# A chunked retention layer followed by a squared-ReLU channel mix: smaller chunks from block 3 on, another form of the token mix in four blocks, and a rewritten instruction order

## The chip, the core and the metric

The kernel runs on one core of a Trainium2 chip. That core has a matrix engine (TensorE, PE in the profile), a vector engine (VectorE, DVE), an activation engine (ScalarE, ACT), a general engine (GpSimd, POOL) and a queue engine (SyncE, SP) that only issues transfers. Each engine executes its own instructions strictly in program order and waits on semaphores for the others. Transfers between HBM and the on-chip memory (SBUF) are moved by 16 DMA engines; they can be issued from POOL (the profile's queue q0, software_dynamic), from SP (q1, hardware_dynamic) and from ACT (q10, hardware_dynamic). TensorE writes its results to PSUM, which has 8 banks.

The metric is the device time of one execution in microseconds. Before the change, three executions took 156.35, 156.45 and 157.85 us, median 156.45.

## What is computed

The first half is a recurrence over 768 tokens for 4 batches and 8 heads of width 64. A 64x64 state is decayed by a head's gamma, gains the outer product of k and v, and is read with q:

```python
gamma = 1.0 - 2.0 ** (-5.0 - np.arange(H))
for t in range(S):
    state = gamma * state + einsum('bhd,bhe->bhde', k[:, :, t], v[:, :, t])
    y[:, :, t] = scale * einsum('bhd,bhde->bhe', q[:, :, t], state)
```

The heads are joined to rows of 512 numbers, x, and the second half is a channel mix in which each token also sees the token before it:

```python
x_prev = x shifted by one token, zero at the start
xk = mu_k * x + (1 - mu_k) * x_prev
xr = mu_r * x + (1 - mu_r) * x_prev
out = sigmoid(xr @ w_r) * (max(xk @ w_k, 0) ** 2 @ w_v)
```

w_k is 512x1024, w_v is 1024x512, w_r is 512x512. Inputs and output are float32; the kernel feeds TensorE with float16.

## The kernel before

The tokens are cut into 12 blocks of 256 tokens; three blocks in a row (0 to 2, 3 to 5, 6 to 8, 9 to 11) belong to one batch and hand a state on. The recurrence is not stepped token by token. Inside a block it is done in chunks: scores of k against q within a chunk (S), a mask (M), the masked scores times v (Y), and what earlier chunks carry over (I and J read the carried states; C makes k times v per chunk, U adds it to the carried state, G applies a whole block's decay).

There are three layouts. Block 0 has 128-token chunks of interleaved tokens. Blocks named in WIDE (1 to 5) have two chunks of 128 tokens. Blocks named in HALF (6 to 11) have four chunks of 64 tokens; their scores are 64x64 pieces that use the four quarters of the matrix array, 32 matmuls a block (line 319), with one mask over the block (line 348) where a wide block has two (line 355). Blocks 0 to 5 turn q and k with 16 transposes of 128 rows each (line 273); blocks 6 to 11 with 32 transposes of 64 rows (line 279).

Every step is a short word in a string, ORDER (lines 23 to 75), which a loop at line 720 walks once. A word's code picks the function, its numbers the block and piece, the letter after ~ the engine (v DVE, a ACT, p POOL, s SP), the digits after @ the PSUM banks. So the order of the words is the order of work on every engine and in every queue; no scheduler moves anything, semaphores only add the waits that data and buffers need.

| word | what it does | line, engine |
|---|---|---|
| lq, lk, lv | load q, k, v of a block (k and v in two halves, except in block 0) | 231, 236, POOL or SP |
| wk, wr, wv | load the weights: wk.1 and wk.0 are the halves of w_k | 700, 703, 707, POOL |
| Tq, Tk; Eq, Ek | transpose q, k; copy the result out of PSUM | 273 or 279 PE; 242 ACT |
| vs | v times the decay factors | 254 DVE |
| S, M, Y, I, J, C, U, G | the chunked recurrence | PE; M, U DVE; G ACT or DVE |
| D | the block's x: PSUM times a decay table into xT | 508 or 515 DVE |
| dx, X | x minus shifted x; mu times that plus shifted x | 530, 539 DVE |
| K, Qa, Qb | w_k product; ReLU; square | 553 or 563 PE; 572, 580, 584 ACT |
| R, s | w_r product; sigmoid | 593 PE; 599 ACT |
| V, O, st | w_v product; times gate; store | 605 PE; 611 DVE; 618 SP |
| z | matmuls on a zero tile | 668, 675 PE |

X.n.w.j makes the j-th quarter of the channels of xk (w = 0) or xr (w = 1). K.n.g needs all four X.n.0.j. Products with w_k take columns 256g to 256g+255 in blocks that stand alone, so K.0.2 and K.0.3 need wk.1 (the second half), K.0.0 and K.0.1 need wk.0. Blocks (3, 4), (6, 7) and (9, 10) are joined for K; the others stand alone.

Buffers are reused in a ring: 4 for q, k and v each, so lv.4 must wait until vs.0 has read block 0's v. Each queue also has 8 semaphores for transfers in flight: a ninth is issued when the first of them has landed.

The order starts with the loads: SP issues the first halves of k and q of block 0; POOL issues the rest of block 0, then v, k, q of block 1, k and q of block 2, wk.1, wk.0, v of block 2, wr, and so on.

Of the kernel before, what the change touches and what calls it, by code (L numbers as in the profile page):

```python
# [22 lines left out]
ORDER = """  # L23
lk.0.0.2~s gy.0 lq.0.2.4~p lv.0~p lq.0.0.2~s lk.0.2.4~p ck.0.0.2~a z.12@6 Tk.0.0.2@0 mu
Tq.0.2.4@1 cq.0.0.2~a z.2@6 Tq.0.0.2@2 Ek.0.0.2~a vs.0~v Eq.0.0.2~a z.2@6 S.0.1.0.2@45
S.0.0.0.2@67 M.0.0.0.2~v Eq.0.2.4~a M.0.1.0.2~v Tk.0.2.4@2 Ek.0.2.4~a C.0@01 U.0.0~a U.0.1
S.0.0.2.4@67 M.0.0.2.4~v I.0@45 S.0.1.2.4@01 mt@3 me M.0.1.2.4~v lv.1~p vs.1~v gy.1~a G.0~a
z.4@2 Y.0 D.0~v lk.1~p Tk.1@0 Ek.1~a C.1@67 U.1.0 lq.1~p z.1@2 Tq.1@1 Eq.1~a dx.0~v X.0.0.0
z.4@2 S.1.1@01 lk.2~p I.1@45 S.1.0@23 M.1.1~v M.1.0~v lq.2~p Tq.2@6 Eq.2~a wk.1~p X.0.0.3 Tk.2@0
X.0.0.2 z.1@1 Y.1 J.1 X.0.0.1 D.1~v U.1.1 Ek.2~a z.1@2 S.2.1@01 S.2.0@23 K.0.2@6 dx.1~v K.0.3@4  # L30
Qa.0.3 Qa.0.2 wk.0~p z.2@5 K.0.1@7 Qa.0.1 K.0.0@5 Qb.0.2 X.0.1.0 X.1.0.2 lv.2~p Qa.0.0 Qb.0.1
X.1.0.3 wr~p X.1.0.1 X.1.0.0 K.1.2@4 lv.3~p G.1~a K.1.1@7 X.0.1.1 vs.2~v Qa.1.2 Qb.1.2 M.2.1~v
Qb.0.0 C.2@5 U.2.0 K.1.0@6 lq.3~p Qa.1.1 X.0.1.2 X.0.1.3 K.1.3@0 Qa.1.3 I.2@45 R.0.1@1 R.0.0@7
s.0.1 M.2.0~v Y.2 Qa.1.0 X.1.1.3 X.1.1.2 Qb.1.0 Tq.3@1 Eq.3~a J.2 X.1.1.0 X.1.1.1 R.1.0@6 s.0.0
# [44 lines left out]
def kernel(  # L79
# [625 lines left out]
    def load_wv(e, h):  # L705
# [59 lines left out]
```

## Time and profile before

The profiled execution took 156.1 us; its span, first to last instruction, was 154.3 us, so 1.8 us lie around it.

| | busy us | share of the span | instructions |
|---|---|---|---|
| PE | 147.3 | 95% | 2316 |
| DVE | 128.1 | 83% | 203 |
| ACT | 99.1 | 64% | 182 |
| POOL | 55.2 | 36% | 67 |

| transfers | packets | MB | share of 16 engines |
|---|---|---|---|
| q0, issued by POOL | 39920 | 14.95 | 75.2% |
| q1, issued by SP | 4512 | 6.69 | 11.9% |

How to read it: the page's part 2 cuts the span into 40 slices of 3.86 us and gives the busy tenths of each engine, so that stages can be told apart. The chain of work goes back from the last instruction through whatever released each step. The timeline gives start, length and name of instructions in order. Matmuls overlap in the records, so PE cost is read here from one piece's start to the next piece's start, not from the recorded length. Transfers have a time of issue and a time of landing; packets of a queue can overlap too, so a queue's share can be over 100% in a short window.

### The profile page before, as it was taken

What the parts mean: (1) busy time and instruction counts of PE and PEld (TensorE: products, weight loads), DVE (VectorE), ACT (ScalarE), POOL (GpSimd) and SP (SyncE); (2) the same over time, 40 slices, a digit from 0 to 9 for tenths busy, and PEclk for the clock granted to TensorE, in tenths of its full rate; (3) what the DMA queues carried; (4) which work ended last, traced back from release to release, by engine and by line L of the source; (5) the groups of instructions that cost most, each with busy time, mean ns of one, the idle gap of its engine ahead of it and who ended that gap; (6) DMA issues with size and microseconds to landing.
All of it is one profiled execution on the core that took longest, in us unless ns stands there. A gap on an engine that the chain in (4) does not pass through costs nothing.

```text
span 154.3 us, 5316 instructions
## 1 busy us (share of the span) xinstructions
PE 147.3 (95%) x2316; PEld 84.2 (55%) x2316; DVE 128.1 (83%) x203; ACT 99.1 (64%) x182; POOL 55.2 (36%) x67
## 2 busy tenths in 40 slices
PE   7979899999999999999999999999998999999991
PEld 3355668558744364556555455546664446455450
DVE  2499999989999999999999999999999996050531
ACT  3559338989872899657572799796411689449330
POOL 7998626788438849108960000000000000000000
PEclk9999999999999999999999999999999999999999
DMA  4999999999999999973999170000300015001435
GB/s 140 283 184 171 204 243 248 166 216 207 190 180 216 219 293 267 188 78 88 305 248 175 12 272 8 0 6 4 138 4 4 0 68 204 0 20 53 155 117 204
DMA packets 44903, 22.29 MB, mean 144 GB/s; under 512 B 36424, under 2 KB 40400, under 8 KB 44880
## 3 DMA queue, kind: packets, MB, share of 16 engines
q0 software_dynamic: 39920, 14.95, 75.2%
q1 hardware_dynamic: 4512, 6.69, 11.9%
q8 instruction: 18, 0.29, 0.8%
q10 hardware_dynamic: 448, 0.32, 0.7%
q14 instruction: 5, 0.04, 0.1%
HBM read 24.31 MB, written 6.29 MB: 198 GB/s over the span
## 4 chain that ended last, share of the span: by engine, by line
PE 42%; DVE 36%; issue 8%; POOL 6%; DMA 5%; ACT 3%; DVEq 0%; POOLq 0%
PE ps L605 13%; PE ps L553 9%; PE ps L593 8%; DVE xk L539 6%; PE ps L563 5%; DVE dx L530 5%; DMA q<-in_q_dram 5%; DVE xr L539 4%; DVE a L355 4%; DVE xT L515 3%; DVE vs L254 3%; DVE tg L420 3%; DVE os L611 2%; POOL k L231 2%; DVE xT L508 2%
## 5 line engine op out<-in xcount | busy, mean ns | idle before, releaser
L605 PE MATMUL ps<-wv,k2s 128*128 128x512 f16 x184 | 44.4, 380 | 0.0
L572 ACT ACTIVATE kr<-ps 128x512 f32<-128x512 f32 x48 | 27.8, 597 | 21.2 <-PE ps L563 11.7
L605 PEld LDWEIGHTS <-k2s 128*128 128x128 f16 x184 | 17.3, 98 | 18.8
L611 DVE SCALAR_TENSOR_TENSOR os<-ps,rs 128x512 f32<-128x512 f32 x23 | 15.1, 684 | 14.4 <-PE ps L605 7.9
L593 PE MATMUL ps<-wr,xr 128*128 128x512 f16 x96 | 23.9, 380 | 0.0
L231 POOL DMA_DIRECT2D v<-in_v_dram x22 | 19.8, 916 | 10.5 <-DVE vs L254 7.9
L563 PE MATMUL ps<-xk,wk 128*128 128x256 f16 x192 | 23.5, 273 | 0.0
L231 POOL DMA_DIRECT2D k<-in_k_dram x22 | 19.6, 905 | 10.5 <-DMA wk<-in_moe_w_k_dram 3.4
L553 PE MATMUL ps<-xk,wk 128*128 128x512 f16 x96 | 22.6, 379 | 0.8 <-DVE xk L539 0.8
L599 ACT ACTIVATE rs<-ps 128x512 f32<-128x512 f32 x24 | 14.1, 602 | 13.5 <-PE ps L593 9.4
L563 PEld LDWEIGHTS <-wk 128*128 128x128 f16 x192 | 18.2, 98 | 4.6 <-DMA wk<-in_moe_w_k_dram 0.5
L539 DVE SCALAR_TENSOR_TENSOR xr<-dx,mu,xT 128x256 f16<-128x256 f32 (+1 forms) x36 | 19.3, 566 | 0.0
L539 DVE SCALAR_TENSOR_TENSOR xk<-dx,mu,xT 128x256 f16<-128x256 f32 (+1 forms) x36 | 18.8, 567 | 0.2
L254 DVE TENSOR_TENSOR vs<-v,csm_sb 128x1024 f16<-128x1024 f32 x12 | 14.6, 1216 | 2.1 <-DMA v<-in_v_dram 2.1
L553 PEld LDWEIGHTS <-wk 128*128 128x128 f16 x96 | 9.0, 98 | 12.1 <-DVE xk L539 1.1
L242 ACT COPY kT<-ps 128x1024 f16<-128x1024 f16 (+1 forms) x13 | 12.2, 951 | 4.4 <-PE ps L279 3.3
L584 ACT ACTIVATE k2s<-kr 128x512 f16<-128x512 f32 x24 | 14.8, 632 | 0.2
L530 DVE TENSOR_TENSOR dx<-xT 128x1024 f32<-128x1024 f32 x12 | 14.6, 1219 | 0.2
L580 ACT ACTIVATE k2s<-kr 128x512 f16<-128x512 f32 x24 | 14.7, 629 | 0.1
L355 DVE TENSOR_TENSOR a<-ps,c_sb 128x1024 f16<-128x1024 f32 (+1 forms) x14 | 14.4, 1062 | 0.0
L242 ACT COPY qT<-ps 128x1024 f16<-128x1024 f16 (+1 forms) x13 | 12.3, 954 | 3.2 <-PE ps L273 2.9
L593 PEld LDWEIGHTS <-xr 128*128 128x128 f16 x96 | 8.7, 98 | 9.7
(67 smaller groups left out, 154.3 us busy)
## 6 DMA issues: line engine op xcount, KB each, us to landing
out_dram<-os SPq DMA_DIRECT2D x23, 256.0 KB, 2.6
v<-in_v_dram POOLq DMA_DIRECT2D x22, 256.0 KB, 7.0
k<-in_k_dram POOLq DMA_DIRECT2D x23, 128.0 KB, 7.4
q<-in_q_dram POOLq DMA_DIRECT2D x11, 256.0 KB, 7.8
wk<-in_moe_w_k_dram POOLq DMA_DIRECT2D x2, 512.0 KB, 10.2
wv<-in_moe_w_v_dram POOLq DMA_DIRECT2D x2, 512.0 KB, 10.0
v<-in_v_dram POOLq DMA_DIRECT2D x1, 512.0 KB, 5.6
wr<-in_moe_w_r_dram POOLq DMA_DIRECT2D x1, 512.0 KB, 13.1
```

The lines of the kernel that those rows point to most:

```text
L231: e.dma_start(out=dst[:, :, i * D : i * D + D], in_=src[:, i * P : i * P + P].rearrange("h p d -> p h d"),)
L242: e.copy(out=out, in_=in_)
L254: e.tensor_tensor(out=VS(n), in0=V32(n).rearrange("p h (i d) -> p i h d", i=2), in1=gks[:, int(half(n) or wide(n)), :, :, None].to_broadca ...
L355: nc.vector.tensor_tensor(out=a_full(n)[:, i, :, j0:j1], in0=pairs(banks("S", n, i, j0))[:, :, j0:j1], in1=(below if wide(n) else causal[: ...
L530: e.tensor_tensor(out=DX(k)[:, :, m * TM + t0 : m * TM + t1], in0=x[:, :, c + t0 : c + t1], in1=x[:, :, c - 1 + t0 : c - 1 + t1], op=ALU.s ...
L539: nc.vector.scalar_tensor_tensor(out=XM[w](k)[:, j, t0:t1], in0=DX(k)[:, j, t0:t1], scalar=mu[:, w * NCO + j : w * NCO + j + 1], in1=x[:, ...
L553: nc.tensor.matmul(banks("K", n, g), lhsT=wk16[:, co, g * P : g * P + P], rhs=XM[0](k)[:, co, :], start=(co == 0), stop=(co == NCO - 1),)
L563: nc.tensor.matmul(pz[:, i, :], lhsT=wk16[:, co, fo * P : fo * P + P], rhs=XM[0](k)[:, co, m * TM + t0 : m * TM + t1], start=(i == 0 and c ...
L572: nc.scalar.activation(out=kr, in_=banks("K", n, g, *u), func=AF.Relu)
L593: nc.tensor.matmul(banks("R", n, tb), lhsT=XM[1](k)[:, co, t : t + P], rhs=wr16[:, co, :], start=(co == 0), stop=(co == NCO - 1),)
L605: nc.tensor.matmul(banks("V", n, tb), lhsT=K2(n)[:, fo, tb * P : tb * P + P], rhs=wv16[:, fo, :], start=(fo == 0), stop=(fo == NFO - 1),)
L611: nc.vector.scalar_tensor_tensor(out=OS(2 * n + tb), in0=banks("V", n, tb), scalar=1.0 / (KSC * KSC), in1=RS(2 * n + tb), op0=ALU.mult, op ...
```

## The change

- HALF becomes blocks 3 to 11 and WIDE blocks 1 and 2: blocks 3, 4 and 5 go from two 128-token chunks to four of 64. WHOLE becomes blocks 0 to 2, so 3, 4 and 5 also take the 32 transposes of 64 rows.
- In blocks 0, 1, 2 and 5 (PARTED) the word dx is gone. For each quarter and each of xk, xr a new word ax lets ScalarE write (1 - mu) times the shifted x, and X computes mu times x plus that. A second small constant, nu = 1 - mu, is made once.
- ORDER is new throughout. Among the loads, v of blocks 0 to 5, 10 and 11 is issued by SP instead of POOL (8 blocks; ~s), and on POOL the order at the start becomes half of k of block 0, q of block 1, half of q of block 0, k of 1, q of 2, k of 2, wk.1, wk.0.
- G of blocks 0, 3 and 9 moves from ACT to DVE, G of block 6 from DVE to ACT, U.9.0 from DVE to ACT. There are 7 z words instead of 9.

```diff
-HALF = (6, 7, 8, 9, 10, 11)
+HALF = (3, 4, 5, 6, 7, 8, 9, 10, 11)
...
-WHOLE = (0, 1, 2, 3, 4, 5)
-WIDE = (1, 2, 3, 4, 5)
+WHOLE = (0, 1, 2)
+WIDE = (1, 2)
+PARTED = (0, 1, 2, 5)
...
 ORDER = """
-lk.0.0.2~s gy.0 lq.0.2.4~p lv.0~p lq.0.0.2~s lk.0.2.4~p ck.0.0.2~a z.12@6 Tk.0.0.2@0 mu
...
+lk.0.2.4~p lq.0.0.2~s cq.0.0.2~a z.8@7 Tq.0.0.2@0 Eq.0.0.2~a lq.1~p lk.0.0.2~s ck.0.0.2~a z.5@1
+Tk.0.0.2@1 Ek.0.0.2~a z.3@2 S.0.1.0.2@23 gy.0 lv.0~s Tk.0.2.4@1 vs.0~v lv.1~s M.0.1.0.2~v mu
+Tq.1@0 C.0@45 vs.1~v lq.0.2.4~p S.0.0.0.2@67 Ek.0.2.4~a M.0.0.0.2~v U.0.0~a lk.1~p z.1@1
+Tq.0.2.4@1 Eq.0.2.4~a z.3@2 I.0@23 S.0.0.2.4@67 U.0.1 Eq.1~a G.0~v M.0.0.2.4~v lq.2~p lk.2~p
+S.0.1.2.4@45 M.0.1.2.4~v Tk.1@1 C.1@67 U.1.0 U.1.1 Y.0 I.1@45 gy.1~a D.0~v wk.1~p Ek.1~a
+S.1.1@67 G.1~a mt@1 me ax.0.0.3 Tq.2@0 S.1.0@23 ax.0.0.1 M.1.1~v ax.0.1.0 ax.0.0.0 M.1.0~v
+X.0.0.3 Tk.2@1 ax.0.1.1 X.0.0.0 Ek.2~a ax.0.0.2 z.4@6 Y.1 J.1 X.0.0.2 wk.0~p X.0.0.1 Eq.2~a
+z.1@6 S.2.1@67 S.2.0@23 K.0.3@0 D.1~v K.0.2@1 M.2.0~v ax.0.1.2 ax.0.1.3 ax.1.0.1 X.1.0.1 lv.2~s
...
     def whole(n):
-        return n in WHOLE or n in WIDE
+        return n in WHOLE
...
+    def kept(n, w, j):
+        return DX(place[n][0])[:, j, w * TM : w * TM + TM]
+
+    def keep(e, n, w, j):
+        x, c = col(n)
+        nc.scalar.activation(
+            out=kept(n, w, j), in_=x[:, j, c - 1 : c - 1 + TM], func=AF.Copy,
+            scale=nu[:, w * NCO + j : w * NCO + j + 1],
+        )
+
     def mixed(e, n, w, j, i=None):
...
+        if n in PARTED:
+            nc.vector.scalar_tensor_tensor(
+                out=XM[w](k)[:, j, 0:TM], in0=x[:, j, c : c + TM],
+                scalar=mu[:, w * NCO + j : w * NCO + j + 1], in1=kept(n, w, j),
+                op0=ALU.mult, op1=ALU.add,
+            )
+            return
```

More of the change, by code (lines that the diff above doesn't have):

```diff
@@ L16 @@
 KUP = 4.0
-HALF = (6, 7, 8, 9, 10, 11)
+HALF = (3, 4, 5, 6, 7, 8, 9, 10, 11)
 EARLY = ((1, 0, 0), (0, 0, 0))
 GROUPS = ((0,), (1,), (2,), (3, 4), (5,), (6, 7), (8,), (9, 10), (11,))
-WHOLE = (0, 1, 2, 3, 4, 5)
-WIDE = (1, 2, 3, 4, 5)
+WHOLE = (0, 1, 2)
+WIDE = (1, 2)
+PARTED = (0, 1, 2, 5)
+WKP = 2
 HEADS = ((0, 1), (3, 2), (4, 5), (7, 6))
 ORDER = """
-lk.0.0.2~s gy.0 lq.0.2.4~p lv.0~p lq.0.0.2~s lk.0.2.4~p ck.0.0.2~a z.12@6 Tk.0.0.2@0 mu
-Tq.0.2.4@1 cq.0.0.2~a z.2@6 Tq.0.0.2@2 Ek.0.0.2~a vs.0~v Eq.0.0.2~a z.2@6 S.0.1.0.2@45
@@ new lines @@
+S.1.1@67 G.1~a mt@1 me ax.0.0.3 Tq.2@0 S.1.0@23 ax.0.0.1 M.1.1~v ax.0.1.0 ax.0.0.0 M.1.0~v
+X.0.0.3 Tk.2@1 ax.0.1.1 X.0.0.0 Ek.2~a ax.0.0.2 z.4@6 Y.1 J.1 X.0.0.2 wk.0~p X.0.0.1 Eq.2~a
+z.1@6 S.2.1@67 S.2.0@23 K.0.3@0 D.1~v K.0.2@1 M.2.0~v ax.0.1.2 ax.0.1.3 ax.1.0.1 X.1.0.1 lv.2~s
+ax.1.0.0 X.1.0.0 ax.1.0.2 X.1.0.2 ax.1.1.1 Qa.0.2 ax.1.0.3 X.1.0.3 ax.1.1.0 lk.3~p K.0.0@4
+Qb.0.2 Qa.0.3 Qa.0.0 ax.1.1.2 K.0.1@1 lq.4~p K.1.3@2 vs.2~v C.2@0 Qa.0.1 Qb.0.0 wr~p K.1.1@3
+X.1.1.1 Qb.0.3 X.0.1.0 lv.3~s U.2.0 M.2.1~v I.2@45 Qb.0.1 Qa.1.1 K.1.2@0 Qa.1.2 X.0.1.1 X.0.1.3
@@ new lines @@
+ax.1.1.3 Qa.1.3 K.1.0@6 X.0.1.2 lq.3~p Qa.1.0 Y.2 X.1.1.2 Tk.3@01 J.2 Ek.3~a X.1.1.0 Tq.4@23
+X.1.1.3 Eq.4~a D.2~v R.0.1@6 ax.2.0.2 ax.2.0.1 R.0.0@7 R.1.0@2 lv.4~s vs.3~v s.0.1 C.3@01
+Tq.3@45 X.2.0.2 X.2.0.1 ax.2.0.0 X.2.0.0 R.1.1@6 ax.2.0.3 X.2.0.3 K.2.3@3 U.3.0~a U.3.1 U.3.2
+lk.4~p U.3.3 vs.4~v s.1.0 Eq.3~a I.3@45 S.3@01 s.1.1 K.2.2@6 Qb.1.1 Qa.2.3 G.3~v C.4@23 s.0.0
+Qb.1.0 Qb.1.2 wv.0~p Qa.2.2 M.3~v wv.1~p ax.2.1.2 K.2.1@7 Tk.4@01 Ek.4~a Y.3 Qa.2.1 U.4.0 U.4.1
+K.2.0@6 U.4.2 I.4@01 U.4.3 G.4~a S.4@23 lk.6~p D.3~v Qb.1.3 M.4~v V.1.0.0@7 V.0.0.0@4 Y.4 Qa.2.0
@@ new lines @@
+Qb.2.0 dx.3~v D.4~v dx.4~v V.1.1.0@6 ax.2.1.1 lq.7~p V.0.1.0@5 ax.2.1.0 lk.5~p V.1.1.1 lq.5~p
+Qb.2.1 Tk.6@23 Ek.6~a X.3.0.2 X.3.0.3 X.3.0.0 Tq.7@01 V.1.0.1 V.0.0.1 X.3.0.1 V.0.1.1 O.1.0
+Eq.7~a O.0.0 Qb.2.3 Tk.5@23 Ek.5~a Tq.5@01 Eq.5~a K.3.3@7 lv.5~s vs.5~v lq.6~p K.3.1@4 Qb.2.2
+K.3.6@2 Qa.3.3 C.5@01 Qa.3.6 O.0.1 O.1.1 Tq.6@67 Eq.6~a K.3.4@5 X.2.1.2 U.5.0 U.5.1 U.5.2 lk.7~p
+X.2.1.1 S.5@23 Qa.3.1 M.5~v Tk.7@67 S.6@01 M.6~v V.2.1.0@4 Ek.7~a I.5@23 Qa.3.4 Qb.3.1 Qb.3.4
+lk.8~p S.7@67 M.7~v ax.2.1.3 K.3.2@5 Qb.3.6 Qa.3.2 V.2.1.1 X.3.1.1 lq.8~p Tq.8@01 lv.6~p X.2.1.0
@@ new lines @@
+Tk.8@67 Qb.3.3 X.2.1.3 Ek.8~a Y.5 Qb.3.2 K.3.7@5 R.2.0@6 D.5~v ax.5.0.2 lv.7~p Eq.8~a lv.8~p
+s.2.0 Qa.3.7 vs.6~v X.3.1.3 R.2.1@2 K.3.0@3 st.0.0 Qa.3.0 st.0.1 X.3.1.2 C.6@01 U.6.0~a
+V.2.0.0@5 X.3.1.0 lk.9~p ax.5.0.3 K.3.5@3 s.2.1 Qb.3.0 U.6.1 U.6.2 vs.7~v Qa.3.5 Qb.3.7 V.2.0.1
+R.3.0@3 U.6.3 ax.5.0.0 O.2.0 st.2.0 G.6~a X.5.0.2 O.2.1 st.2.1 R.4.1@2 s.3.0 X.5.0.0 lq.11~p
+s.4.1 C.7@67 I.6@01 U.7.0 U.7.1 U.7.2 ax.5.0.1 X.5.0.1 X.5.0.3 U.7.3 Tk.9@45 Ek.9~a lq.9~p
+V.3.1.0@3 R.4.0@2 I.7@45 Y.6 vs.8~v G.7~a s.4.0 D.6~v lv.10~s dx.6~v K.5.0@7 K.5.3@6 lq.10~p
@@ new lines @@
+Qb.3.5 V.4.0.0@2 ax.5.1.3 C.8@01 Y.7 D.7~v dx.7~v U.8.0 X.6.0.0 U.8.1 Qa.5.0 Qb.5.0 st.1.1
+st.1.0 X.6.0.3 X.6.0.2 ax.5.1.0 U.8.2 V.3.0.0@7 V.3.0.1 O.3.0 V.4.1.0@4 V.4.1.1 ax.5.1.1 O.4.1
+ax.5.1.2 X.6.0.1 Qa.5.3 R.3.1@5 s.3.1 Qb.5.3 K.5.2@1 Qa.5.2 Qb.5.2 K.5.1@5 Qa.5.1 V.3.1.1 O.3.1
+lv.11~s I.8@01 st.3.1 X.5.1.3 S.8@67 Tq.9@45 lk.10~p Eq.9~a V.4.0.1 M.8~v K.6.3@3 Qb.5.1 st.3.0
+Qa.6.3 Tq.10@45 Eq.10~a Tk.10@67 O.4.0 Ek.10~a Y.8 lv.9~p V.5.0.0@2 V.5.0.1 Tq.11@45 Eq.11~a
+S.10@67 vs.9~v D.8~v C.9@01 X.5.1.0 K.6.2@3 X.5.1.2 X.5.1.1 M.10~v Qa.6.2 st.4.1 K.6.6@4 K.6.1@3
@@ new lines @@
+K.6.4@5 vs.10~v Qb.6.2 X.6.1.2 X.6.1.1 Qa.6.1 Qa.6.6 R.5.0@3 U.9.0~a lk.11~p U.9.1 U.9.2 Qb.6.1
+s.5.0 dx.8~v O.5.0 U.9.3 X.6.1.3 Qa.6.4 Qb.6.4 V.5.1.0@4 G.9~v R.5.1@0 s.5.1 V.5.1.1 O.5.1
+Tk.11@67 C.10@23 S.9@01 Ek.11~a K.6.5@5 Qa.6.5 Qb.6.5 X.6.1.0 X.8.0.1 M.9~v K.6.0@6 Qa.6.0
+R.6.0@5 s.6.0 U.10.0 U.10.1 R.7.0@4 s.7.0 R.6.1@5 s.6.1 U.10.2 U.10.3 I.10@67 X.8.0.0 S.11@01
+st.4.0 I.9@23 X.8.0.2 X.8.0.3 Qb.6.6 R.7.1@4 s.7.1 K.6.7@5 M.11~v Qa.6.7 K.8.0@4 Qa.8.0 vs.11~v
+Y.9 D.9~v Y.10 D.10~v C.11@01 K.8.2@4 G.10~v U.11.0 dx.10~v dx.9~v X.9.1.2 Qb.6.3 X.8.1.2
@@ new lines @@
+K.8.1@5 Qb.6.7 Qb.6.0 V.6.1.0@2 V.7.0.0@3 V.6.0.0@6 V.6.0.1 K.8.3@7 Qa.8.1 X.9.0.2 Qa.8.2
+V.7.1.0@4 V.7.1.1 V.7.0.1 X.9.0.0 Qa.8.3 Qb.8.0 Qb.8.1 O.6.0 U.11.1 Qb.8.2 X.9.0.1 V.6.1.1
+X.9.0.3 Qb.8.3 V.8.0.0@5 K.9.3@6 Qa.9.3 X.8.1.3 X.9.1.3 K.9.0@7 K.9.2@6 X.9.1.1 Qa.9.0 K.9.6@7
+X.9.1.0 O.6.1 K.9.4@2 Qa.9.6 st.5.0 O.7.0 K.9.5@7 Qa.9.5 R.9.0@3 K.9.1@7 st.5.1 O.7.1 R.10.0@4
+U.11.2 I.11@01 Qb.9.3 Qa.9.2 K.9.7@6 st.6.1 X.8.1.1 Qb.9.2 Qa.9.1 Qb.9.1 Qa.9.7 X.8.1.0 st.7.0
+V.8.1.0@7 Qb.9.6 R.8.0@6 Y.11 s.9.0 V.8.0.1 Qb.9.0 V.9.1.0@3 Qa.9.4 st.7.1 Qb.9.5 R.9.1@2 s.8.0
@@ new lines @@
+D.11~v Qb.9.4 V.8.1.1 R.10.1@6 dx.11~v R.8.1@0 X.11.1.1 X.11.0.0 X.11.1.0 s.8.1 X.11.0.3
+V.10.0.0@1 X.11.0.1 X.11.0.2 st.6.0 X.11.1.2 O.8.0 X.11.1.3 V.9.0.0@0 K.11.1@5 s.10.0 Qb.9.7
+s.9.1 Qa.11.1 K.11.3@4 V.10.1.0@5 st.8.0 O.8.1 K.11.0@2 st.8.1 V.9.0.1 V.9.1.1 Qa.11.3 Qb.11.3
+O.9.1 Qa.11.0 Qb.11.0 O.9.0 st.9.0 K.11.2@4 Qa.11.2 Qb.11.2 V.10.0.1 st.9.1 O.10.0 st.10.0
+R.11.1@4 s.10.1 Qb.11.1 V.10.1.1 O.10.1 st.10.1 V.11.0.0@6 R.11.0@7 s.11.0 V.11.0.1 s.11.1
+O.11.0 st.11.0 Vc.11.1.0@7 Oc.11.1.0 Vc.11.1.1@4 Oc.11.1.1 sc.11.1.0~s sc.11.1.1~a
@@ L164 @@
     mu = const.tile([P, 2 * NCO], F32, name="mu")
+    nu = const.tile([P, 2 * NCO], F32, name="nu")
     wk16 = const.tile([P, NCO, dff], F16, name="wk16")
@@ L663, in copy_mu @@
         nc.scalar.copy(out=mu, in_=banks("mt")[:, 0 : 2 * NCO])
+        if PARTED:
+            nc.scalar.activation(out=nu, in_=mu, func=AF.Copy, scale=-1.0, bias=1.0)
     def zeros(e, count):
@@ L698, in load_wk @@
     def load_wk(e, h):
-        f = slice(h * dff // 2, (h + 1) * dff // 2)
+        f = slice(h * dff // WKP, (h + 1) * dff // WKP)
         nc.gpsimd.dma_start(out=wk16[:, :, f], in_=wks[:, :, f])
@@ L713 @@
         "S": scores, "M": masked, "C": state, "U": summed, "G": decayed, "I": inter_off, "Y": intra, "J": inter_on,
-        "D": yout, "dx": differ, "X": mixed, "K": keys, "Qa": relued, "Qb": squared, "R": gate,
+        "D": yout, "dx": differ, "ax": keep, "X": mixed, "K": keys, "Qa": relued, "Qb": squared, "R": gate,
         "s": opened, "V": values, "O": result, "st": store, "gy": powers, "wk": load_wk,
```

49 lines of the change are left out of this document (removed).

## The prediction

> **What bounds the kernel now.** I read the slices first, to see when each engine is full.
>
> ```profile
> PE   7979899999999999999999999999998999999991
> DVE  2499999989999999999999999999999996050531
> ACT  3559338989872899657572799796411689449330
> DMA  4999999999999999973999170000300015001435
> ```
>
> A slice is 3.86 us. Transfers fill the first 17 slices (66 us), VectorE nearly everything to slice 32, TensorE everything from slice 5. Next the timeline of PE where its solid stretch begins, and POOL's:
>
> ```profile
> 17.24 0.64 PE L273 MATMUL ps<-c_sb,q 128*64 128x128 f16 x16 [0.70 <-DMA q<-in_q_dram]
> ...
> 20.45 1.92 PE L563 MATMUL ps<-xk,wk 128*128 128x256 f16 x16
> 22.21 0.59 PE L675 MATMUL ps<-zero 128*128 128x512 f16 x2
> 22.80 3.67 PE L563 MATMUL ps<-xk,wk 128*128 128x256 f16 x32
> ```
>
> ```profile
> 20.09 0.88 POOL L231 DMA_DIRECT2D k<-in_k_dram  x1 [1.35 <-DMA wk<-in_moe_w_k_dram]
> 23.04 0.88 POOL L231 DMA_DIRECT2D k<-in_k_dram  x1 [2.07 <-DMA wk<-in_moe_w_k_dram]
> ```
>
> K.0.2 and K.0.3 start at 20.45, after wk.1 has landed (19.79); then zeros bridge until wk.0 lands (22.75) and K.0.1 starts at 22.80. From there the next pieces follow each other to 151.16: the idle marks on PE add up to under 1 us. So two things set the time: **when wk.0 lands, and how much PE work comes after it**. The 3.1 us behind PE's end (gate, store) stay as they are.
>
> **Smaller chunks: PE loses 2.8 us.** I sum, for a block's Tq, Tk, S, C, Y, I and J, the time from each piece's start to the next piece's start.
>
> ```profile
> 34.57 0.64 PE L273 MATMUL ps<-c_sb,k 128*64 128x128 f16 x16
> 44.85 0.44 PE L279 MATMUL ps<-c_sb,q 64*64 64x64 f16 x32
> ```
>
> These two lines are one turned block each: 0.57 us to the next piece when wide, 0.28 to 0.43 when half. All pieces: wide blocks 3, 4 and 5 take 2.95, 2.99 and 2.73 us; half blocks with the same place in their batch (6, 7, 8) take 1.90, 1.85 and 2.08. Saved: 8.67 - 5.83 = 2.84 us, all behind 22.8 and on the path, since PE is solid there.
>
> **VectorE loses 5 us.** Four dx at 1.22 (-4.9); in three blocks one mask of 1.21 instead of two (-3.6); six more U at 0.42 (+2.5); three D as 2 x 0.69 instead of 1.22 (+0.5); G net two more at 0.42 (+0.8); U.9.0 goes (-0.4). DVE is as full as PE to 117 us, so it must lose about what PE loses if PE's saving is to count; it does.
>
> **ScalarE gains 10.5 us.** 32 ax. The trace has no Copy of 128x256 with a scale; Copies with a scale take 348 ns for 64 columns (G) and 391 for 128 (the decay table), so 477 for 256 by that slope, and 0.38 as the engine advances, since its instructions overlap by 0.1 (G: four in 1.06). 32 x 0.38 = 12.2; two G fewer, -2.1; U.9.0, +0.4. It has 99 of 154 now. The new wait is X for its ax, which stands behind Qa, Qb and E in ACT's line; behind an X on DVE wait the next X, vs.2 and M.2.1. From 20 to 40 us ACT is busy 16.5 of 20; ax of blocks 1 and 2 (16, 6.1) less G.1 and G.3 (2.1) makes 20.5. So ACT is 0.5 us short there if block 0's keys start on time, up to 2 if its order fits badly; if they start late, ax.0 and most of ax.1, ordered before Qa.0.2, are done in the wait and this costs nothing.
>
> **The loads: wk.0 comes later.** POOL's transfers run one after another; landing to landing before: half k of block 0 0.61, lq.1 1.44, lk.1 1.15, lq.2 1.37, lk.2 2.43, wk.1 2.59, wk.0 2.96, and half q of block 0 as half of lq.1, 0.72. Now these eight are POOL's first: 10.31 us to wk.1, 13.27 to wk.0. v of a block took 1.86, 2.46, 1.84 and 2.26, mean 2.1. In the old order only v of 0 and 1 stood before wk.0. Now SP issues v of 0, 1, 2 and 3 without waiting for any compute, and 4 and 5 after vs.0 and vs.1: 12.6 us of transfers that are under way while wk is. What SP's small pieces cost the trace does not show: 33 ns per piece per engine (its q and k of block 0, 512 bytes each, 243 GB/s) would give 4.2 us for the 2048 pieces of a halved v block; k's pieces on POOL go at 13 ns, which gives 1.7. I take 2.1, POOL's own v.
>
> Do the two queues add up or share? Transfers between 58.6 and 59.8 us, when stores from SP met k from POOL:
>
> ```profile
> q0 software_dynamic: 774, 0.10, 130.1%
> q1 hardware_dynamic: 103, 0.19, 41.5%
> ```
>
> That is 645 k packets and 86 store packets per us. Alone, k runs at 1226 per us (10 to 11 us) and stores at 210 (90 to 92 us). 645/1226 + 86/210 = 0.53 + 0.41 = 0.94: they share, SP gets about 0.4. [...]
>
> With SP's share h, POOL's packets starting at 4.1 us and SP's v at 4.6 (when its q and k are through): wk.0 lands at 4.1 + 13.27/(1-h), v of 1 at 4.6 + 4.2/h. From v of 1, DVE must do, by start-to-start steps before, vs.1 1.23, M.0.0 0.6, U 0.34, G 0.36, two M 1.2, two U 0.66, D.0 1.15, two M 2.27, four X 1.66 = 9.5 us to K.0.3, and K.0.3 and K.0.2 1.75 more to K.0.0.
>
> | h | wk.0 | v of 1, + 11.25 | K.0.0 | against 22.80 |
> |---|---|---|---|---|
> | 0.25 | 21.8 | 21.4, 32.6 | 32.6 | +9.8 |
> | 0.35 | 24.5 | 16.6, 27.8 | 27.8 | +5.0 |
> | 0.40 | 26.2 | 15.1, 26.4 | 26.4 | +3.6 |
> | 0.45 | 28.2 | 13.9, 25.2 | 28.2 | +5.4 |
> | 0.50 | 30.6 | 13.0, 24.2 | 30.6 | +7.8 |
>
> 0.4 is the best for the new order, and either side is worse. I take 0.45, between the measured 0.4 and an equal share: **+5.4**. Later loads are not late: wr needs 5.8 us after wk.0 (lk.3, lq.4, wr), and PE has 7 us between K.0.0 and R.0.1.
>
> **The sum.** 156.1 (the profiled execution) - 2.8 + 5.4 = 158.7; that execution is 0.35 under the median, so **159.0** beside the runs shown. Its own range: 156.9 + 0.35 = 157.2 at h = 0.4, 161.3 at 0.5, up to 163.5 at 0.25 or with v pieces dearer than 2.1. One per cent, what a measurement of this kernel can tell from no change, is 154.9 to 158.0.
>
> **Rivals.**
>
> *The loads fit in, and it is faster.* v on SP could ride where POOL's small packets leave the engines' data path empty: k moves only 155 GB/s, stores alone 381. Then wk.0 and v of 1 land as before, K.0.0 starts at 22.8, and PE's 2.8 us come through: 153.3 + 0.35 = 153.7, with ACT's 0.5 154.2. It decides if wk.0 lands before 24.4. Against it stands the 0.94. Chance 0.25, 152.8 to 154.9.
>
> *Nearly balanced.* h close to 0.4 with POOL at its best pace, or PE stalls of the old order (under 1 us) also gone: 156 to 157.5. Chance 0.14, within 1%.
>
> *SP starves.* From 54 to 55 us, with k in full flow, SP's first store moved 21 packets against 761. If each 256-byte piece of v takes a turn of its own and lets 7.5 (the 58.6 to 59.8 ratio) to 36 k packets by, 2048 pieces take 12 to 60 us while POOL has work; POOL has 26.8 us of it that waits for no v but block 0's (to wv.1). v of 1 lands at 27 to 35, the keys start 15 to 23 us late, and the time is 169 to 177. For it: a lone store took longer beside loads.
>
> ```profile
> out_dram<-os SPq DMA_DIRECT2D x2, 256.0 KB, 5.0
> ```
>
> That is the median from issue to landing between 54 and 60 us; between 90 and 92, with no loads, it is 2.8. Against it: the 0.4 share afterwards. [...] Chance 0.13 with everything above 163.5.
>
> **Chances.** The forecast 0.48, faster 0.25, balanced 0.14, starved 0.13. Slower by over 1%: 0.48 + 0.13 = 0.61; within: 0.14; faster: 0.25. The range goes from 152.8 to 165: it leaves out most of the starved case and a little at the fast end.
>
> **What would show it.** Landing of wk.0 near 28 and an idle PE before K.0.0 prove the shared engines; PE waiting for vs.1 or X instead means the starved side. From K.0.0 to PE's end the time should be 128.4 - 2.8 = 125.5 us; more means that ACT or DVE became the bound, to be seen as PE waiting for X or for a freed bank. The prediction is wrong if wk.0 lands before 24.4.

## The result, and the profile after the change

The changed kernel takes **173.48 us** (median; 172.55 to 175.63), beside 157.15 us for the kernel before: ratio 1.10, 95% interval 1.089 to 1.113. It is slower by 16.3 us; 159.0 was forecast and 165.0 was the end of the range. Its profiled execution took 173.35 us with a span of 171.6; before it was 156.1 and 154.3. So 17.3 us are to be found. Executions more than 1.5% above the fastest of the same kernel count as a slower state, and the times of the versions below are medians of the others, which makes 173.4 for the changed kernel.

The slices of the changed kernel (now 4.29 us each), with the granted clock:

```profile
PE   7828869894996989788999699999999999999991
DVE  2243894799296899696999979999989990492431
ACT  3506475999399547696989267687672448918630
PEclk9985587998799999999999999999999999999999
DMA  5999999999999999899599904203000023003153
```

Three things are new. TensorE has holes in the first 23 slices, where it was solid from slice 5 on. Transfers fill 23 slices almost without a break (98 us), where before they filled 17 (66 us) and came in bursts after that; the last load packet starts at 99.8 instead of 86.5. And the granted clock, which was 1.0 in the kernel before, is low in slices 3 to 7 and in 10 and 11. The next fence is the timeline of PE about the first products; x16, x8 and so on count matmuls, and the bracket gives the idle time in front and what ended it.

```profile
29.55 1.92 PE L585 MATMUL ps<-xk,wk 128*128 128x256 f16 x16
31.68 1.05 PE L585 MATMUL ps<-xk,wk 128*128 128x256 f16 x8 [0.21 <-DMA wk<-in_moe_w_k_dram]
33.09 1.91 PE L585 MATMUL ps<-xk,wk 128*128 128x256 f16 x16 [0.36 <-ACT kr L594]
...
42.31 4.25 PE L615 MATMUL ps<-wr,xr 128*128 128x512 f16 x12 [2.21 <-ACT dx L545]
```

The first product starts at 29.55 instead of 20.45, and K.0.0 waits for wk.0. At 42.31 R.0.1 waits 2.2 us; the bracket names a scaling that ended then, but wr landed at 42.26 as well, and in three of the runs below the same wait is marked wr. Its first seven matmuls run at clock 0.5, 427 ns apart instead of 216: another 1.5 us. POOL's timeline shows the landings of wk.1 and wk.0 as the end of POOL's own waits, 28.3 and 31.6 against 19.8 and 22.8 before:

```profile
28.53 0.87 POOL L236 DMA_DIRECT2D k<-in_k_dram  x1 [2.44 <-DMA wk<-in_moe_w_k_dram]
31.92 0.75 POOL L731 DMA_DIRECT2D wv<-in_moe_w_v_dram  x1 [2.52 <-DMA wk<-in_moe_w_k_dram]
```

Then comes what no step of the prediction had. Further on in PE's timeline pieces are cut in two, and what lies between is marked "issue": the engine waited for nothing that the profile shows.

```profile
55.71 0.28 PE L447 MATMUL ps<-qT,tg 64*64 64x64 f16 x10 [1.70 <-issue]
...
62.18 0.32 PE L284 MATMUL ps<-c_sb,k 64*64 64x64 f16 x15 [0.59 <-issue]
...
67.55 1.69 PE L575 MATMUL ps<-xk,wk 128*128 128x512 f16 x7 [0.29 <-issue]
...
72.38 0.22 PE L284 MATMUL ps<-c_sb,k 64*64 64x64 f16 x3 [0.91 <-issue]
```

Two more follow at 77.75 and 95.87. From the start of the last matmul in front to the next one they are 1.89, 0.78, 0.66, 1.10, 1.37 and 1.98 us, 7.8 in all; the kernel before has none. I counted TensorE's instructions (matmuls and weight loads, by start time) up to each: 1473, 1729, 1985, 2241, 2497 and 3265. The first five are **256 apart**, the last is three times 256 further on. And each stall ends 2.3 to 2.7 us after the start of a packet of 16384 bytes in queue q8, "instruction". The first of these packets, in the transfers from 53 to 55.5 us:

```profile
q0 software_dynamic: 2394, 0.41, 211.2%
q8 instruction: 1, 0.02, 2.3%
```

The columns are packets, MB and the time of the packets as a share of the 16 engines. Loads fill all engines twice over (211.2%, packets overlap), and the one packet of q8 goes among them. That such a packet brings TensorE's next 256 instructions is read from counts: 20 of them came for the 5204 matmuls and weight loads of the changed kernel, 260 a packet, and 18 for the 4632 of the kernel before, 257 a packet; and the stalls stand 256 or a multiple of it apart. The kernel before takes its 18 packets without a stall; the changed kernel stalls at six of 20.

The 17.3 us are split by two marks: the first product starts 9.1 us later (29.55 against 20.45), from there to PE's end it takes 138.6 us instead of 130.7 (+7.9), and the tail is 0.3 longer. In the +7.9 stand the stalls (about 7.3 beyond the normal step), wr (2.2), the slow clock (1.5) and K.0.1's wait (0.4), together 11.4, against smaller chunks (-2.8, the size forecast). That makes 8.6, 0.7 more than was measured; what gives it back I cannot name.

### The profile page after: what moved, and what is told of

Same layout as the page of the kernel before. It is cut to its first block, busy times and chain, and to the rows that moved or that the text cites. A ratio compares the mean times of both kernels' runs of the same rounds, so it can differ in the third digit from the quotient of the medians.

```text
span 171.6 us, 5909 instructions
## 1 busy us (share of the span) xinstructions
PE 151.1 (88%) x2602; PEld 85.3 (50%) x2602; DVE 124.1 (72%) x206; ACT 110.6 (64%) x208; POOL 41.6 (24%) x52
## 4 chain that ended last, share of the span: by engine, by line
PE 70%; DMA 10%; ACT 6%; issue 5%; DVE 4%; POOL 3%; ACTq 0%; DVEq 0%; POOLq 0%
PE ps L627 24%; PE ps L615 12%; PE ps L575 12%; DMA k<-in_k_dram 10%; PE ps L585 8%; PE ps L284 3%; ACT dx L545 2%; PE ps L447 2%; PE ps L468 2%; PE ps L372 1%; POOL k L236 1%; POOL q L241 1%; PE ps L324 1%; ACT kr L594 1%; PE ps L692 1%
## 5 line engine op out<-in xcount | busy, mean ns | idle before, releaser
L627 PEld LDWEIGHTS <-k2s 128*128 128x128 f16 x184 | 17.3, 98 | 20.1 <-issue 1.9
L615 PE MATMUL ps<-wr,xr 128*128 128x512 f16 x96 | 25.0, 398 | 2.2 <-ACT dx L545 2.2
L575 PE MATMUL ps<-xk,wk 128*128 128x512 f16 x96 | 23.2, 380 | 0.3 <-issue 0.3
L259 DVE TENSOR_TENSOR vs<-v,csm_sb 128x1024 f16<-128x1024 f32 x12 | 14.6, 1217 | 8.3 <-DMA v<-in_v_dram 8.3
L513 DVE TENSOR_TENSOR xT<-ps,gy_sb 128x512 f32<-128x512 f32 x18 | 12.4, 690 | 9.5 <-PE ps L447 8.1
L615 PEld LDWEIGHTS <-xr 128*128 128x128 f16 x96 | 9.5, 102 | 14.3 <-DMA wr<-in_moe_w_r_dram 2.3
L545 ACT ACTIVATE dx<-xT,nu 128x256 f32<-128x256 f32 x32 | 14.7, 506 | 2.7 <-DVE xT L520 2.3
L425 DVE TENSOR_TENSOR tg<-ps,tg 128x256 f16<-128x256 f32 x26 | 11.0, 422 | 4.1 <-ACT tg L247 1.6
L241 POOL DMA_DIRECT2D q<-in_q_dram x12 | 10.5, 890 | 10.6 <-PE ps L284 7.5
L353 DVE TENSOR_TENSOR a<-ps,c_sb 128x1024 f16<-128x1024 f32 x9 | 11.0, 1219 | 2.4 <-PE ps L324 2.4
```

The costliest lines, as they stand in the source:

```text
L259: e.tensor_tensor(out=VS(n), in0=V32(n).rearrange("p h (i d) -> p i h d", i=2), in1=gks[:, int(half(n) or wide(n)), :, :, None].to_broadca ...
L545: nc.scalar.activation(out=kept(n, w, j), in_=x[:, j, c - 1 : c - 1 + TM], func=AF.Copy, scale=nu[:, w * NCO + j : w * NCO + j + 1],)
L575: nc.tensor.matmul(banks("K", n, g), lhsT=wk16[:, co, g * P : g * P + P], rhs=XM[0](k)[:, co, :], start=(co == 0), stop=(co == NCO - 1),)
L615: nc.tensor.matmul(banks("R", n, tb), lhsT=XM[1](k)[:, co, t : t + P], rhs=wr16[:, co, :], start=(co == 0), stop=(co == NCO - 1),)
L627: nc.tensor.matmul(banks("V", n, tb), lhsT=K2(n)[:, fo, tb * P : tb * P + P], rhs=wv16[:, fo, :], start=(fo == 0), stop=(fo == NFO - 1),)
```

## The experiments

Theory A has two parts: v on SP delays the weights, and TensorE's instruction packets wait behind loads, which small matmuls turn into stalls. The rivals are the scalings on ScalarE, the order by itself, and, for the stalls, the number of small matmuls alone. All numbers together; "first" is the start of the first product, "stretch" the time from there to PE's end, "stalls" the gaps of 0.5 us and more behind the first product that stand at the count of a 256-block and end 2.2 to 2.8 us after the start of its packet.

| kernel | time us | ratio (95%) | first | stretch | stalls |
|---|---|---|---|---|---|
| before | 157.2 | | 20.5 | 130.7 | 0 |
| after | 173.4 | 1.089 to 1.113 | 29.6 | 138.6 | 7.8 |
| a1: after, v on POOL | 169.8 (two: 168.7, 170.9) | | 23.2 | 142.7 | 11.0 |
| a2: after, v in 512-byte pieces | 175.8 | 1.113 to 1.132 | 32.3 | 137.6 | 8.9 |
| b1: before, v on SP | 167.8 | 1.066 to 1.077 | 29.6 | 132.9 | 0.5 |
| b2: before, scalings | 165.2 | 1.049 to 1.061 | 22.8 | 137.9 | 0 |
| c1: after, no late loads | 168.8 | 1.061 to 1.083 | 31.1 | 131.0 | 2.8 |
| c2: after, differences | 174.6 | 1.110 to 1.124 | 28.8 | 140.5 | 8.7 |
| c3: before, small chunks | 169.7 | 1.071 to 1.084 | 22.3 | 143.2 | 0 |
| c4: a1, no late loads | 160.5 (one) | | 23.4 | 132.1 | 4.1 |
| d1: after, wide chunks | 170.7 | 1.080 to 1.098 | 30.1 | 135.7 | 1.8 |
| d2: d1, v on POOL | 163.6 | 1.037 to 1.051 | 23.5 | 134.8 | 1.2 |
| d3: d2, differences | 165.3 | 1.049 to 1.064 | 24.4 | 136.7 | 1.2 |

The kernel before, run beside them, took 156.5 us with a1 to b2, 157.6 with c1 to c4 and 156.4 with d1 to d3.

### a1: v back on POOL in the changed kernel

```diff
-... gy.0 lv.0~s ... lv.1~s ... lv.2~s ... lv.11~s
+... gy.0 lv.0~p ... lv.1~p ... lv.2~p ... lv.11~p
```

> The changed kernel with v of all blocks issued by POOL at the same places of the order; nothing else differs. Theory 1 (v on SP holds up w_k): wk.0 lands near 23 us as before the change, because POOL then has the same 13.3 us plus two v blocks ahead of it, K.0.0 starts at 23 to 24, and PE's stalls within a piece between 55 and 96 us are the only loss left: 153 to 157 us. Theory 2 (the new order itself is slow, whatever queue v takes): 165 us or more. If the stalls within pieces (7.3 us in the changed kernel) come from instruction blocks that wait behind loads, they shrink here, as the loads end some 10 us sooner; if they come from the density of small matmuls alone, they stay at about 7 us.

The loads came back as expected: wk.1 at 20.35, wk.0 at 23.27, wr at 30.81, first product at 23.18. The time did not: 169.8, 3.6 less than the changed kernel where 16 to 20 less were expected. Of the 6.4 us that the first product gained, the profiled execution lost 4.2 again in the stretch, where the stalls grew to 11.0 us:

```profile
49.62 0.37 PE L447 MATMUL ps<-qT,tg 64*64 64x64 f16 x10 [3.35 <-issue]
...
91.78 1.60 PE L627 MATMUL ps<-wv,k2s 128*128 128x512 f16 x5 [3.57 <-issue]
```

They stand at 256-blocks as in the changed kernel (1473 and 3265 here, which stalled there too; 1217 and 1985 are the others, and at 1985 the bracket names a VectorE instruction, though TensorE goes on 2.6 us after the packet as at the rest). The clock is 0.5 for 6.8 us from within the first of them and for 3.4 us behind the second. That the loads were early again and little came of it is why the stalls became the main question.

### b1: v on SP in the kernel before

```diff
-lv.0~p ... lv.1~p ... lv.5~p ... lv.10~p ... lv.11~p
+lv.0~s ... lv.1~s ... lv.5~s ... lv.10~s ... lv.11~s
```

> The kernel before with v of blocks 0 to 5, 10 and 11 issued by SP; nothing else differs. Theory 1: 13.3 us of POOL's transfers and 14.3 us of SP's (block 0 at 1.95, three blocks at 4.1) lie ahead of wk.0, so it lands at 4.1 + 27.6 = 31.7 us instead of 22.75 and the end moves by 9 to 11 us: 165 to 168. Theory 2: within 2 us of before.

167.8 us, ratio 1.07: this edit alone costs 11.3 us. wk.0 landed at 31.06, and 9.2 us of the loss lie ahead of the first product (29.6 against 20.5); the stretch is 2.2 longer. On the way PE waits for q of block 2, and the matmuls behind that wait run at half clock:

```profile
24.40 1.06 PE L273 MATMUL ps<-c_sb,q 128*64 128x128 f16 x16 [3.89 <-DMA q<-in_q_dram]
25.25 1.07 PE L273 MATMUL ps<-c_sb,k 128*64 128x128 f16 x16
```

This order, with its wide chunks, has a stall too. The first line is the kernel before, the second and third are b1 at the same instructions, whose packet started at 76.60:

```profile
68.50 0.50 PE L279 MATMUL ps<-c_sb,q 64*64 64x64 f16 x32
...
78.34 0.33 PE L279 MATMUL ps<-c_sb,q 64*64 64x64 f16 x18
78.97 0.31 PE L279 MATMUL ps<-c_sb,q 64*64 64x64 f16 x14 [0.30 <-issue]
```

The queue change is a loss in either order (a1 against the changed kernel shows it in the new one, 3.6 us); the new order does not cause it.

### a2: the same v in larger pieces

```diff
-"lv": load(v, V32, True),
+"lv": load(v, V32, False),
```

> The changed kernel with every block of v loaded by one transfer of 1024 pieces of 512 bytes instead of two of 1024 pieces of 256 bytes. The tokens of a block then lie in another order than the masks and decays assume, so it computes another function; the work on every engine is the same. If a piece costs a turn whatever its size (31 to 33 ns), a block of v takes 2.1 us instead of 4.1: v of 1 lands near 13 us, all six early blocks of v are through by 30 us, wr lands near 36 instead of 42, and the time falls by 3 to 6 us. If bytes set the price, no landing moves by more than 1 us and the time stays near 173.

This was half right: wr landed at 37.54 instead of 42.26 and R.0.1 no longer waits, but wk.0 landed at 31.84, not earlier, and the time is 175.8. By the counts of packets, SP had moved some five blocks of v besides block 0's by 28 us, where it had moved three and a third by 32 us in the changed kernel. With cheaper pieces SP did not leave POOL more room, it ran further ahead.

### b2: the scalings in the kernel before

```diff
-dx.2~v X.2.0.2
+ax.2.0.0 ax.2.0.1 ax.2.0.2 ax.2.0.3 ax.2.1.0 ax.2.1.1 ax.2.1.2 ax.2.1.3 X.2.0.2
```

> The kernel before with dx of blocks 0, 1, 2 and 5 replaced by eight ax each at the same place, and X reading them; nothing else differs. If VectorE was on the path in the first 60 us, 4.9 us less of it shows as 1 to 2 us; if ScalarE becomes the bound there (16.5 busy of 20 us, 6 more to do), it is slower by 1 to 3 us. By theory 1 it has no part in the 17 us: 154.5 to 159.

165.2 us, not expected. The largest wait shows in ACT's timeline and PE's:

```profile
36.46 3.30 ACT L545 ACTIVATE dx<-xT,nu 128x256 f32<-128x256 f32 x8 [0.47 <-DVE xT L520]
39.67 0.99 ACT L247 COPY kT<-ps 128x1024 f16<-128x1024 f16 x1
```

```profile
40.71 0.64 PE L278 MATMUL ps<-c_sb,k 128*64 128x128 f16 x16 [3.28 <-ACT kT L247]
```

Eight scalings in one place hold ACT for 3.3 us; the copy Ek.3 stands behind them, and Tk.4 waits for the bank that Ek.3 must empty. Behind that wait, from 41.9, the granted clock is 0.5 for 3.4 us. The rest lies elsewhere: the first product starts 2.3 us later, and another wait, for DVE at 77.9, is 1.8 us. So this run prices a block of eight in ACT's line and not the changed kernel's arrangement, where they are spread.

### c2: the changed kernel without scalings

```diff
-me ax.0.0.3 Tq.2@0 S.1.0@23 ax.0.0.1 ...
+me dx.0~v Tq.2@0 S.1.0@23 ...
```

> The changed kernel with the 32 ScalarE scalings of shifted rows taken out again and the differences of blocks 0, 1, 2 and 5 on VectorE, each where the first scaling of its block stood. If the scalings cost nothing on the path, as the chain of the changed kernel says, the time stays at 172 to 176 us. If ScalarE with 110.6 us of work is part of the loss, it falls by 3 us or more, to 164 to 170 us.

174.6 us: the scalings are no part of the loss. In d2 against d3, where less else disturbs, they look like a gain of 1.7 us (163.6 against 165.3), but the two intervals overlap.

### c1 and c4: no loads for blocks 6 to 11

```diff
-lk.6~p ... lq.7~p ... lv.6~p ... lk.11~p
+
```

> The changed kernel with q, k and v of blocks 6 to 11 not loaded (their buffers keep blocks 2 to 5, so the second half computes other numbers with the same instructions). In the changed kernel TensorE stands still six times in the middle of a piece, 7.8 us in all at 55.7, 62.2, 67.6, 72.4, 77.8 and 95.9 us, each time 256 instructions further on, each time just after a 16384-byte packet of the instruction queue. Theory A: that packet, the next 256 instructions, waits behind the data transfers in the same 16 DMA engines (it starts 2.8 to 6.1 us after the block before is begun, against -1.2 to 0.8 us once the loads are over, after 104 us). Then the stalls from 62 us on are gone here, the packets start within about 1 us of the block's begin, and the time is 165 to 169 us. Rival B: small matmuls use up 256 instructions faster than a refill can come in any case. Then the stalls stay and the time is 172 to 175 us.

> The changed kernel with every v issued by POOL (which gave 171.6 us) and in addition q, k and v of blocks 6 to 11 not loaded. There the stalls in the middle of pieces were 1.8, 3.5, 1.9 and 3.8 us, and the granted clock was 0.5 for 6.8 and 3.4 us after two of them. Theory A (instruction packets wait behind loads): at least the last two go, with the slow clock behind the last; 158 to 164 us. Rival B (too many small matmuls for any refill): 169 to 172 us. A value under 157 would say that v's queue and these stalls are the whole loss; one above 160 with no stall left leaves something else to find.

This decides between the two explanations of the stalls. c1 has the same matmuls in the same order, and every stall from 62 us on is gone; its two stalls are at 50.2 and 55.1 us, while the loads of blocks 3 to 5 and of w_v are still under way. Its transfers from 69.5 to 72 us are one packet:

```profile
q8 instruction: 1, 0.02, 2.5%
```

The table follows five blocks in both kernels: when TensorE starts the last instruction ahead of the block before, when the packet starts, and when TensorE is through with what it has.

| block from | after: block before begun, packet, used up, goes on | c1: block before begun, packet, used up |
|---|---|---|
| 1729 | 53.82, 59.90, 61.40, 62.18 | 53.43, 56.18, 60.74 |
| 1985 | 61.40, 64.81, 66.89, 67.55 | 60.74, 59.68, 65.47 |
| 2241 | 66.89, 69.96, 71.27, 72.38 | 65.47, 65.44, 69.36 |
| 2497 | 71.27, 75.30, 76.38, 77.75 | 69.36, 70.16, 73.39 |
| 3265 | 89.94, 93.52, 93.89, 95.87 | 85.58, 86.58, 89.53 |

With loads in front the packet starts 3.1 to 6.1 us after the block before is begun; without them 1.1 us ahead to 2.8 after, and 1.0 at most from 59 us on. The 256 instructions meanwhile last 3.7 to 5.7 us, counted from where TensorE goes on. **The packet waits behind the loads.** For these five stalls the count of small matmuls alone is refuted as a cause: the same ones run through in c1.

Loads are not needed for every stall. In d1, d2 and d3 one remains at block 3265 where no load is under way, only SP's stores (353 to 360 packets between the block's begin and the packet): the packet starts 1.9 us late and the block lasts 3.0 us. What all runs share is the time between the packet's start and the restart, 2.2 to 2.8 us. In these runs a block that was used up sooner than that after its packet had started stalled, behind loads and behind stores. An estimate from these numbers (1.0 and 2.2): with a packet 1.0 us late, as in c1, a block must still last 3.2 us or more.

Without late loads the stretch is 131.0 in c1 and 132.1 in c4, and c4's remaining 4.1 us of stalls stand among the early loads (the packet of the longer one starts at 45.9). The waits of c4, total, number and longest:

```profile
PE ps L446 <- issue: 2.8, 1, 2.8
...
PE ps L584 <- ACT kr L593: 1.0, 1, 1.0
...
PE ps L371 <- issue: 0.8, 1, 0.8
```

c1 is 168.8 us and c4 160.5, both inside the ranges for theory A. Between c1 and c4 lies v's queue alone: 7 to 8 us (7.1 between the profiled executions). One thing in c1 is not explained: its first product starts 1.5 us later than in the changed kernel though the early loads are the same, and the granted clock is 0.5 ahead of it for 6.8 us instead of 3.4.

### c3: small chunks alone in the kernel before

```diff
-S.3.1@45 S.3.0@67 ... U.3.1 ... M.3.1~v ... M.3.0~v ... I.3@23 ... Y.3 ... J.3
+U.3.1 U.3.2 U.3.3 ... I.3@67 S.3@45 M.3~v ... Y.3
```

> The kernel before with the 64-token chunks and 64x64 transposes of blocks 3, 4 and 5 alone: every load, every queue and the difference form as before. My first working gave -2.8 us of matrix work, so about 153.7 us. With theory A of the instruction packets it is not faster: between 35 and 75 us the kernel before starts such a packet 2.6 to 3.9 us after the block before is begun and has 1.4 to 2.7 us in hand; with the smaller matmuls a block of 256 lasts 3.3 to 4.5 us instead of 6.5, so two to four stalls of 0.5 to 2 us appear there: 155 to 161 us.

169.7 us, further off than either expectation, and for another reason: no stall stands at a block's end. Instead PE waits for the small chunks' own chain (10.5 us of waits in the stretch, the largest of them here), and the granted clock is 0.5 for 6.8 and 3.4 us:

```profile
PE ps L563 <- ACT qT L242: 2.0, 1, 2.0
PE ps L605 <- DVE xT L508: 1.9, 1, 1.9
PE ps L279 <- DVE tg L420: 1.2, 1, 1.2
PE ps L319 <- ACT kT L242: 1.1, 1, 1.1
```

It seems that the old order gives the four sums U of a block, and I, S, M and Y in a row behind them, no room. The run says that this edit needs an order made for it; it does not test the theory, since a TensorE that waits uses up its instructions more slowly.

### d1, d2, d3: wide chunks in the new order

```diff
-I.3@45 S.3@01 ... M.3~v ... Y.3
+I.3@45 S.3.1@01 M.3.1~v ... S.3.0@01 ... M.3.0~v ... Y.3 J.3
```

> The changed kernel with blocks 3, 4 and 5 back in two 128-token chunks and 128-row transposes; loads, queues, scalings and order stay. If the smaller chunks were a gain of 2.84 us of matrix work and nothing else, this is 176 us. By theory A (instruction packets that come late because loads are in front of them, and 256 small matmuls that are over in 3.3 to 4.5 us instead of 6.5 us) most of the stalls at 55.7, 62.2 and 67.6 us go with them, those in blocks 6 and 7 after 72 us may stay: 169 to 173 us, stalls of 2 to 5 us in all instead of 7.8.

> The same with every v issued by POOL. v on SP cost 11.3 us in the kernel before by itself, and 7.0 us between the two kernels without late loads; the stalls of 1.8 and 3.5 us in blocks 3 and 4 should be gone, and the slow clock behind the second: 160 to 165 us. If v on SP were the only loss that counts, and the stalls only its consequence, it would be 171 us as with the small chunks.

> The same again with differences instead of scalings: what is left of the change is its order (and G and U on other engines). Scalings cost nothing in the changed kernel's order (175.2 against 173.5 us with and without differences), so this is within 2 us of the run with scalings. If it is at 156 to 158 us, the order is no loss by itself; if it stays above 160, the order of the first products and the late loads has its own price.

d1 and d2 came out inside the ranges given, d1 with 1.8 us of stalls, a little under what was expected; d3 lies 1.7 us above d2, inside the 2 expected, and above 160. With 128-token chunks a block of 256 instructions lasts 5.8 to 9.6 us between 45 and 85 us in d1, and the stalls of that part are gone although the packets still start up to 2.9 us late. Small chunks under v on SP cost 2.6 us in all (173.4 against 170.7, intervals that overlap), with v on POOL 6.2 (a1 against d2). The stalls that they bring, 6.0 and 9.8 us more than with wide chunks, eat up what they save. d1 to d3 also carry waits of their own, from the two halves of S sharing banks; in d2 they are

```profile
PE ps L338 <- DVE a L361: 1.1, 2, 0.7
...
PE ps L448 <- DVE a L361: 0.9, 1, 0.9
...
PE ps L485 <- DVE a L361: 0.3, 1, 0.3
```

2.3 us together. So d2 less these and less 1.2 of stalls has a stretch of 131.3, within 0.6 of the kernel before. By this sum the order costs next to nothing there. It costs ahead of it: with all of v on POOL the first product still starts at 23.2 to 24.4 instead of 20.5, since it stands behind S.2.1, which waits for the copy of block 2's q in ACT's line. This is a1:

```profile
22.62 0.62 PE L337 MATMUL ps<-qT,kT 64*128 64x128 f16 x16 [0.98 <-ACT qT L247]
```

No version tried beats the kernel before; even c4, which leaves out half of the loads, does not.

## Why the prediction was wrong

**Smaller chunks: right in size, wrong that it counts.** Blocks 3 and 5 take 2.0 and 1.8 us where they took 2.95 and 2.73, as worked out; block 4 holds a stall and cannot be read. Without the stalls and the two waits named (1.2 for wr in c1, 1.0 for K.0.1 in c4) the stretches of c1 and c4 are 127.0 and 127.1, under the 127.9 that -2.84 gives. The step that failed is "on the path, since PE is solid there". A solid TensorE was taken to stay solid; that its instructions must arrive in time was not asked, and the term for it stood at nothing; the runs put 7.8 us of stalls there, which c1 takes away from 62 us on by leaving out loads alone. The kernel before shows those packets too, between 35 and 75 us as much as 3.9 us after the block before is begun. At the tightest the packet starts at 66.25 and the block is used up at 68.64, 2.4 us later; as the stalls end 2.2 to 2.8 us after a packet's start, nothing is in hand there, and b1 stalls at that very block. Elsewhere in that stretch the wide chunks leave 3.3 us or more between the two. Small chunks use that margin up: the 256 instructions that stall first last 3.3 us (50.48 to 53.82), and the kernel before took 6.3 us for the same count.

**From K.0.0 to PE's end: 125.5 forecast, 136.4 measured** (31.68 to 168.12). Of the 14.7 us between the 158.7 of the sum and 173.35, these are 10.9; 3.5 lie ahead of K.0.0 (31.68 instead of 28.2) and 0.3 in the tail. I had said that more would mean ACT or DVE as the bound. It was neither: PE waits for ACT come to 0.4 us there beside the 2.2 at R.0.1.

**VectorE and ScalarE: right.** DVE 124.1 us busy where 123.1 was worked out, ACT 110.6 where 109.6 was. The one price that the trace of before did not show, the scaling, was near:

```profile
L545 ACT ACTIVATE dx<-xT,nu 128x256 f32<-128x256 f32 x32 | 14.7, 506 | 2.7 <-DVE xT L520 2.3
```

506 ns against 477, and 0.40 as the engine advances (b2's eight in 3.30 us) against 0.38.

**The loads: right mechanism, mis-sized.** They do share the engines, and wk.0 came at 31.64 instead of 28.2. The term that was too small is the share h: by the prediction's own formula 31.64 means h = 0.52, where 0.45 was taken, and its row for 0.5 gives 30.6. By packets the queues moved nearly one for one; from 18 to 20 us, POOL's queue and SP's:

```profile
q0 software_dynamic: 841, 0.13, 86.4%
q1 hardware_dynamic: 723, 0.18, 70.2%
```

The price of v, 2.1 us a block, was too low as well. A piece of 256 bytes from SP is recorded with 31 ns, which makes 4.0 us for 2048 pieces on 16 engines; that is an upper estimate, since records overlap. At 2.1 the six early blocks would have been through by about 30 us at equal shares; by 32 us SP had moved 6832 such pieces, three and a third blocks besides block 0's. a2, with cheaper pieces, landed wk.0 no earlier (31.84), so this price did not set that landing. It set how long SP went on beside POOL, and "Later loads are not late" fell with it: wr landed 10.6 us after wk.0, not 5.8, and R.0.1, which starts right behind that landing, had waited 2.2 us.

**Left out, but hidden here:** the new order's own start. With v on POOL the first product starts at 23.18 instead of 20.45 (a1), 2.7 us that the sum had at nothing. In the changed kernel they do not show, because K.0.0 starts when wk.0 has landed.

**The rivals.** "Fit in" and "nearly balanced" needed wk.0 before 24.4 and near 26; it came at 31.6. "SP starves" gave 169 to 177 us and the time is in it, but not by its mechanism: v of block 1 landed at 15.69, not at 27 to 35, and the first products waited for wk and not for v. Nearly equal counts of packets (841 to 723 from 18 to 20 us) are what the queues moved. No rival had the stalls.

**What stays open.** What small chunks would bring in an order that suits them, with instructions in time, was not measured by itself: c3 and d1 to d3 add waits of their own. Nor is it shown why a1's packets start later (up to 7.7 us) than those of the changed kernel; only that loads are in front of them. The later first product of c1 is open too. Nothing was done to the instruction queue itself.

## What to carry to other kernels

Count instructions, not only busy time: where an edit turns few matmuls into many small ones while loads or stores fill the DMA engines, look up the packets of the instruction queue (16384 bytes here) and ask how long the instructions that one of them brings last (256 of TensorE here, 3.3 us for those that stalled first) against the time until the next one is there (at the stalls here it started 1.9 to 6.2 us after the block before was begun, and TensorE went on 2.2 to 2.8 us after that); a stall marked "issue" in the middle of a piece, 256 instructions after another, was its sign. A transfer moved to a second queue did not get room of its own here: it shared the engines, 841 packets to 723 in 2 us, with the transfers that had been ahead of it, so what the first products need must not meet what is only needed later. And where a removed delay brings little back, as in a1, look for a second limit before the first theory is dropped.

## What the runs showed of the hardware

- TensorE ran out of instructions: six stalls, 7.8 us in all, in the changed kernel. Packets of the instruction queue start between 1.1 us ahead of and 1.0 us after the block before is begun when no loads are in front (c1 from 59 us to 120), and 2.2 to 6.2 us after it for the blocks that stalled amid loads in the changed kernel, a1, a2, b1, c1, c2 and c4; behind SP's stores 1.9 us were enough for blocks of 3.0 us (d1 to d3). TensorE goes on 2.2 to 2.8 us after the packet's start in all of them; a stall lasts 0.5 to 3.8 us.
- The recorded length of a small piece is not what it costs the engines. Alone in them, POOL's loads ran at 1226 pieces of 128 bytes per us, about 690 of 256 and about 200 of 1024; on 16 engines that is 13, 23 and 80 ns a piece. The recorded lengths are longer (32, 41 and 98 ns), since records overlap, and they rise less from 128 to 256 bytes than the price does. For SP's pieces of v, which were never alone, only recorded lengths can be given: 31 ns for 256 bytes and 40 for 512.
- In several places half clock set in during a pause of TensorE or just behind it: in 3.9 us of waiting in b1, in and behind stalls of 3.5 and 3.8 us in a1, but also in the 2.2 us before R.0.1 in the changed kernel; the 3.0 us of c4 (45.6 to 48.6) had none. The matmuls behind the pause were twice as far apart (427 ns against 216 in R.0.1), and the slow stretches lasted 3.4, 6.8, 10.2 or 13.7 us (10.2, 3.4 and 3.4 in the changed kernel).
